# A pair's block sums of v, copied out of PSUM and spread over v's rows in the pair's first or second slot

## The chip, the cores and the metric

The kernel runs on one core of one Trainium2 chip. A time is the device time of one execution in microseconds (us), and the figure that counts is the median of several executions.

The engines are named as the profile names them: PE (TensorE, matrix multiplications; PEld is its loading of weights), DVE (VectorE), ACT (ScalarE), POOL (GpSimd) and SP (SyncE, which only issues DMA transfers here). Each takes its instructions in the order in which the program lists them. An instruction that needs another engine's result waits at the head of its queue, and all that stands behind it on that engine waits too.

## The reference

Attention comes first: each query sees a window of its neighbours and, beside them, one summary of each block of 32 keys. A block's value summary is the mean of its 32 rows of v. Two feed-forward stages follow.

```
k_sum = k.reshape(B, H, nb, block, D).max(axis=3)      # block = 32
v_sum = v.reshape(B, H, nb, block, D).mean(axis=3)
...
scores_all = np.concatenate([scores_l_m, scores_s], axis=-1)
...                                                     # softmax -> a
v_all = np.concatenate([v, v_sum], axis=2)
return np.matmul(a, v_all)                              # _attn_ref
...
h = x @ w_in                                            # _moe_ref, 512 -> 2048 -> 512
g = np.where(h > 0.0, h, np.exp(np.minimum(h, 0.0)) - 1.0)
x = g @ w_out
...                                                     # _moe2_ref: each token to one of 8 experts
```

The shapes are 2 batches, 8 heads, 768 tokens and 64 elements of a head; 1536 tokens of 512 elements go through the feed-forward stages.

## The kernel before

Attention is cut into **pairs** p of two heads and 384 tokens. There are 16 pairs, and each is worked in two **units** u of three query blocks of 64: units 2p and 2p+1. A **slot** `sl` of the main loop starts unit u = sl, so a pair has a first slot (even, `sl % GPP == 0`) and a second slot (odd). The order of instructions is the order in which the loop's body is written; no scheduler changes it.

The steps of a unit u are these. I write S3, T3 and so on for step and unit.

- S(u): `pe_s`, L280, PE: scores of 12 matmuls into PSUM; the keys `kw` and queries `qt` must be there.
- max(u): `dve_max`, L294, DVE: adds the mask and finds the row maxima, three instructions with a read of the result behind each.
- exp(u): `act_exp`, L301, ACT: three exponentials with their row sums.
- norm(u): L307 and L308 on DVE (the reciprocal of the row sums), then L309 on POOL, which multiplies.
- T(u): `pe_t`, L316, PE: three transposes of the result, one slot later.
- pT(u): `act_t`, L320, ACT: copies these out of PSUM, two slots after S(u).
- O(u): `pe_o`, L328, PE: probabilities times values, two slots after S(u). The values are the pair's tile `vw`: rows 0 to 95 are the windows of v, loaded by DMA (L187), and rows 96 to 119 are the block sums.
- copy of O(u): `act_o`, L339, ACT.

The block sums of a pair p come in four steps: `prep_va` (L222, DVE) sums blocks of v; V(p), `pe_va` (L230, PE), transposes the sums at the pair's first slot; `fin_va` (L236, ACT) copies them out of PSUM into `vs`, with the division by 32; `load_vs` (L242, POOL) spreads `vs` over the six windows of `vw`.

The first nine slots are the **prologue** (LAG = 9). In slots 0 to 7 the four pairs of the first 384 tokens are worked by attention alone, with some matmuls on the identity (`busy`, L884) between them. The last of these slots' work, O6 and O7, stands in slot 8, which already has the first matrix product of the feed-forward stage, `mm1(0, 0)` (L440), between S8 and O6. From slot 9 on each slot holds attention and feed-forward work.

In a prologue slot PE runs: S(u), V(p) if the slot is even, O(u-2), two `busy` matmuls, T(u-1). The lines that call the two steps in question, for pairs 1 to 3, are these; pair 0 has its own call in slot 1, and from pair 4 on `load_vs` is a DMA from a `vs` that is there already.

```
1200            if 0 < p < NPAIR and sl % GPP == 0:
1201                fin_va(p)                          # behind exp(u), ahead of the copy of O(u-2)
...
1245            if 0 < p < NPAIR and sl % GPP == 0:
1246                load_vs(p)                         # behind norm(u)
```

Of the kernel before, what the change touches and what calls it, by code (L numbers as in the profile page):

```python
# [22 lines left out]
NPAIR = NH // 2  # L23
# [26 lines left out]
def build(tc, cap, qT, kT, vT, vP, wi, wo, wg, wgT, wx, out):  # L50
# [6 lines left out]
    with ctx:  # L57
# [89 lines left out]
        GPP = QPT // GRP  # L147
# [84 lines left out]
        def fin_va(p):  # L232
            t, pr = divmod(p, NPAIR)
            if t % 2 == 0:
                VS[p] = apool.tile([P, P], F32, tag=f"vs{pr}", bufs=1, name=f"vs{p}")
                nc.scalar.mul(out=VS[p][WK:KEYS], in_=PS.pop(("v", p))[WK:KEYS], mul=1.0 / BLK)  # L236
            else:
                VS[p] = VS[p - NPAIR]

        def load_vs(p):  # L240
            if p < NPAIR:
                nc.gpsimd.tensor_copy(  # L242
                    out=VW[p][WK:KEYS], in_=VS[p][WK:KEYS].unsqueeze(1).to_broadcast([NSUM, QPT, P]))
                return
            nc.sync.dma_start(
                out=VW[p][WK:KEYS], in_=VS[p][WK:KEYS].unsqueeze(1).to_broadcast([NSUM, QPT, P]))
# [51 lines left out]
        def act_exp(u):  # L298
            sc, st = SC[u], ST[u]
            for gi in range(GRP):  # L300
                nc.scalar.activation(  # L301
                    out=sc[:, gi], in_=sc[:, gi], func=AF.Exp, bias=st[:, 0, gi : gi + 1],
                    scale=-1.0, accum_out=st[:, 1, gi : gi + 1])

        def norm(u):
            sc, st = SC[u], ST.pop(u)
            nc.vector.tensor_scalar(out=st[:, 2], in0=st[:, 1], scalar1=1e-9, scalar2=None, op0=ALU.add)  # L307
            nc.vector.reciprocal(out=st[:, 2], in_=st[:, 2])  # L308
            nc.gpsimd.tensor_tensor(  # L309
                sc, sc, st[:, 2].unsqueeze(2).to_broadcast([P, GRP, KEYS]), op=ALU.mult)  # L310
# [638 lines left out]
        for sl in range(total):  # L949
            n = sl - LAG  # L950
            u, p = sl, sl // GPP
# [245 lines left out]
            if u < NU:  # L1197
                dve_max(u)
                act_exp(u)
            if 0 < p < NPAIR and sl % GPP == 0:  # L1200
                fin_va(p)
            if sl == 0:
                prep_va(0)
# [38 lines left out]
                dve_o(u - 2)  # L1242
            if u < NU and not dense:
                norm(u)
            if 0 < p < NPAIR and sl % GPP == 0:
                load_vs(p)
            if sl in (LAG - 3, LAG - 2):
                w_conv([("i", sl - LAG + 3)], (2,))
# [291 lines left out]
```

## Time and profile before

| what | value |
|---|---|
| median of 3 runs | 494.66 us (494.08 to 495.25) |
| profiled execution, its own time | 495.4 us |
| its span, first to last instruction | 493.7 us |
| PE busy | 468.8 us (95%) |
| DVE busy | 333.7 us (68%) |
| ACT busy | 262.7 us (53%) |
| POOL busy | 189.5 us (38%) |
| mean granted clock of TensorE | 0.996 |

The profile is of one execution. The busy shares are averages over stages of different kinds, and the change touches only the first 30 us, so what matters is the timelines of that stretch, engine by engine: when each instruction starts, how long it runs, and in brackets how long its engine stood idle before it and what ended that.

### The profile page before, as it was taken

To read this page: it belongs to the slowest core of one execution; us is meant where nothing else is said; L and a number is where in the kernel's file an instruction comes from. 1 tells how busy PE (TensorE), PEld (TensorE's weight loads), DVE (VectorE), ACT (ScalarE), POOL (GpSimd) and SP (SyncE) were. 2 spreads that over 40 slices of the span, in tenths; PEclk is the share of its full clock that TensorE was granted. 3 is DMA by queue.
4 is the path that set the end of the run, shared out by engine and by line. 5 is a ranking of instruction groups with operands and counts; after the bars stand their busy time and mean duration, and the time that the engine had idled before them with its cause. 6 is when DMAs were issued, how large, how long until landed. Compare 5 with 4: busy or idle time off the path is not lost. (4 is left out here: it accounts for less than half of the span.)

```text
span 493.7 us, 9010 instructions
## 1 busy us (share of the span) xinstructions
PE 468.8 (95%) x2982; PEld 390.5 (79%) x2982; DVE 333.7 (68%) x889; ACT 262.7 (53%) x661; POOL 189.5 (38%) x197
## 2 busy tenths in 40 slices
PE   6999999999999999999999999999989999999983
PEld 5655555788888899998999899989768889798762
DVE  4869999666755477885279889756695846265550
ACT  4756446777665555564333333425734856376440
POOL 5632444555333358886233233123523040120430
PEclk9999999999999999999999999999999999999998
DMA  8996774433522433486010100106628875376570
GB/s 256 289 306 183 222 219 119 123 105 85 161 82 88 145 113 116 141 322 231 0 65 2 61 5 1 65 0 218 184 69 280 260 245 179 109 238 194 155 254 13
DMA packets 33729, 72.85 MB, mean 148 GB/s; under 512 B 4156, under 2 KB 9212, under 8 KB 33648
## 3 DMA queue, kind: packets, MB, share of 16 engines
q1 hardware_dynamic: 31888, 66.71, 42.7%
q0 software_dynamic: 1760, 5.19, 3.4%
q8 instruction: 34, 0.56, 0.5%
q14 instruction: 47, 0.39, 0.2%
HBM read 61.88 MB, written 9.70 MB: 145 GB/s over the span
## 5 line engine op out<-in xcount | busy, mean ns | idle before, releaser
L447 PE MATMUL h<-xT,Wi 128*128 128x384 f32 x672 | 130.3, 340 | 0.0
L492 PE MATMUL acc<-Wo,g 128*128 128x512 f32 x504 | 127.0, 396 | 0.2 <-POOL g L472 0.2
L447 PEld LDWEIGHTS h<-xT,Wi 128*128 128x128 f32 x672 | 118.0, 188 | 5.8 <-issue 1.9
L472 POOL TENSOR_TENSOR g<-e,g 128x384 fp32r<-128x384 f32 x55 | 65.0, 1182 | 127.9 <-ACT g L466 127.9
L492 PEld LDWEIGHTS acc<-Wo,g 128*128 128x128 f32 x504 | 92.9, 188 | 17.9 <-POOL g L472 0.7
L459 DVE SCALAR_TENSOR_TENSOR e<-e,h 128x384 f32<-128x384 f32 x64 | 35.3, 552 | 50.8 <-ACT e L455 47.4
L454 ACT ACTIVATE e<-h 128x384 f32<-128x384 f32 x64 | 31.5, 492 | 57.7 <-PE h L447 54.0
L466 ACT CAST g<-e 128x384 fp32r<-128x384 f32 x56 | 28.8, 514 | 45.8 <-DVE e L459 45.8
L684 DVE TENSOR_TENSOR E<-rawq,E 128x512 fp32r<-128x512 f32 x70 | 46.5, 706 | 8.5 <-ACT E L674 7.2
L816 PE MATMUL bh<-xbq,E 128*128 128x256 f32 (+1 forms) x288 | 43.5, 303 | 3.4 <-DVE tabs L1388 1.4
L674 ACT CAST E<-rawq 128x512 fp32r<-128x512 f32 x75 | 42.3, 617 | 6.5 <-DMA rawq<-wx 3.4
L816 PEld LDWEIGHTS bh<-xbq,E 128*128 128x128 f32 x288 | 41.2, 188 | 5.8 <-issue 1.7
L301 ACT ACTIVATE sc<-sc,st 128x120 f32<-128x120 f32 x96 | 36.7, 385 | 13.9 <-DVE st L294 13.8
L309 POOL TENSOR_TENSOR sc<-sc,st 128x360 f32<-128x360 f32 x32 | 27.9, 872 | 38.1 <-DVE st L308 26.0
L805 PE MATMUL y<-E,g 128*128 128x512 f32 x168 | 41.7, 393 | 0.0
L554 DVE CUSTOM_DVE_ANT_0 dot<-a,wgb 128x512 f32<-128x512 f32 x48 | 40.0, 887 | 0.0
L805 PEld LDWEIGHTS y<-E,g 128*128 128x128 f32 x168 | 30.6, 188 | 5.7
L455 ACT ACTIVATE e<-e 128x384 f32<-128x384 f32 x64 | 33.6, 525 | 2.0
L294 DVE CUSTOM_DVE_ANT_0 sc<-S,masks 128x120 f32<-128x120 f32 x96 | 21.5, 278 | 16.4 <-PE S L269 9.2
L320 ACT COPY pT<-T 120x384 f32<-120x384 f32 x32 | 15.3, 479 | 30.7 <-PE T L316 29.4
L824 DVE TENSOR_TENSOR g<-e,g 128x256 fp32r<-128x256 f32 (+1 forms) x24 | 11.3, 470 | 25.3 <-ACT g L823 21.0
L721 POOL DMA_INDIRECT out<-ys,sidx x6 | 6.3, 1052 | 48.2 <-ACT ys L720 46.7
(251 smaller groups left out, 694.4 us busy)
## 6 DMA issues: line engine op xcount, KB each, us to landing
rawq<-wx SPq DMA_DIRECT2D x88, 256.0 KB, 3.9
rawi<-wi SPq DMA_DIRECT2D x16, 512.0 KB, 3.7
rawo<-wo SPq DMA_DIRECT2D x16, 512.0 KB, 6.2
vw<-vP SPq DMA_DIRECT2D x16, 288.0 KB, 3.0
qt<-qT SPq DMA_DIRECT2D x16, 192.0 KB, 3.7
vt<-vT SPq DMA_DIRECT2D x8, 384.0 KB, 3.1
out<-xg SPq DMA_DIRECT2D x12, 256.0 KB, 4.8
x2d<-a SPq DMA_DIRECT2D x12, 256.0 KB, 4.2
```

The source lines that it names most:

```text
L301: nc.scalar.activation(out=sc[:, gi], in_=sc[:, gi], func=AF.Exp, bias=st[:, 0, gi : gi + 1], scale=-1.0, accum_out=st[:, 1, gi : gi + 1])
L447: nc.tensor.matmul(HP[t, f][:, 0:TT], lhsT=w[:, s, c * P : (c + 1) * P], rhs=xT[t][:, xs, c, :], start=c == 0 and n == 0, stop=c == NCC - ...
L454: nc.scalar.activation(out=e, in_=HP[t, f][:, 0:TT], func=AF.Exp)
L455: nc.scalar.activation(out=e, in_=e, func=AF.Relu, bias=1.0, scale=-1.0)
L459: nc.vector.scalar_tensor_tensor(out=e, in0=e, scalar=-1.0, in1=h[:, 0:TT], op0=ALU.mult, op1=ALU.max)
L472: eng.tensor_tensor(g[:, 1], EP.pop((t, f)), g[:, 0].bitcast(F32), op=ALU.subtract)
L492: nc.tensor.matmul(accp[tb], lhsT=g[:, s, tb * P : (tb + 1) * P], rhs=w[:, ws], start=f % FPG == 0 and n == 0, stop=f % FPG == FPG - 1 and ...
L554: nc.vector.tensor_tensor_reduce(out=junk, in0=x2[t * BPT + tb], in1=WGB[e // 2][:, e % 2], scale=1.0, scalar=0.0, op0=ALU.mult, op1=ALU.a ...
L674: (nc.vector.tensor_copy if m in vec else nc.scalar.copy)(EW[k][m][:, 0], raw_of(k, m))
L684: (nc.gpsimd if m in pool else nc.vector).tensor_tensor(w[:, 1], raw, w[:, 0].bitcast(F32), op=ALU.subtract)
L805: nc.tensor.matmul(ys[b], lhsT=g[:, s, b * P : (b + 1) * P], rhs=w[:, ws], start=f == 0 and n == 0, stop=f == 7 and n == 2)
L816: nc.tensor.matmul(h[:, 0:nt], lhsT=EW[k][half * NCC + c][:, ws, fc * P : (fc + 1) * P], rhs=xb[:, s, c, 0:nt], start=n == 0, stop=n == 3 ...
```

## The change

For pairs 1, 2 and 3 both calls get the condition `sl % GPP == 1` in place of `sl % GPP == 0`. The pair's first slot keeps V(p).

```diff
-            if 0 < p < NPAIR and sl % GPP == 0:
+            if 0 < p < NPAIR and sl % GPP == 1:
                 fin_va(p)
...
-            if 0 < p < NPAIR and sl % GPP == 0:
+            if 0 < p < NPAIR and sl % GPP == 1:
                 load_vs(p)
```

No instruction is added or removed, and no DMA is moved: for these pairs `fin_va` is one instruction on ACT and `load_vs` one on POOL. Three of each move.

On POOL, around the first slot of pair 1 (`sc` is a unit's probabilities, `kw` the keys of the pair after, `vw` the pair's values), the order before is:

```order
L309 TENSOR_TENSOR sc_272<-sc_272,st_273 128x360
L242 COPY vw_198<-vs_280 24x768
L309 TENSOR_TENSOR sc_328<-sc_328,st_329 128x360
L197 COPY kw_377<-kt_238 128x6x64
L199 COPY kw_377<-kt_238 128x6x32
L216 COPY kw_377<-ks_380 128x6x24
L309 TENSOR_TENSOR sc_366<-sc_366,st_367 128x360
```

The three products on L309 are norm 2, norm 3 and norm 4. At the same place on POOL, the changed kernel has:

```order
L309 TENSOR_TENSOR sc_272<-sc_272,st_273 128x360
L309 TENSOR_TENSOR sc_325<-sc_325,st_326 128x360
L242 COPY vw_198<-vs_333 24x768
L197 COPY kw_375<-kt_238 128x6x64
L199 COPY kw_375<-kt_238 128x6x32
L216 COPY kw_375<-ks_378 128x6x24
L309 TENSOR_TENSOR sc_366<-sc_366,st_367 128x360
```

The spread over `vw` has gone behind norm 3, the product of the pair's second unit; the copies of keys now follow it.

PE's order is the same in both kernels. In the changed one, around the start of slot 4 (V(2), then O2, which reads the `vw` above, then T3 and S5), with the engines that each waits for:

```order
L230 MATMUL V_355<-ident,va_126 120x128 [waits DVE_49]
L328 MATMUL O_359<-pT_357,vw_198 64x64 [waits DMAHW2_49,Activation_49,Pool_49]
L328 MATMUL O_359<-pT_357,vw_198 64x64 x5
L884 MATMUL warm<-ident 128x128 x2
L316 MATMUL T_389<-ident,sc_325 120x128 [waits PE_49]
L316 MATMUL T_389<-ident,sc_325 120x128 x2
L280 MATMUL S_393<-kw_282,qt_225 64x120 [waits DVE_49,PE_49]
```

What moved is what O2's wait for POOL stands for: the spread is POOL's instruction ahead of norm 3 before, and the one behind it now. T3, which waits for norm 3, stands behind O2 in both and no longer has a wait of its own for POOL.

On ACT the copy `vs` (L236) leaves its place between exp 2 and the copy of O0 and stands between exp 3 and the copy of O1; likewise for pairs 2 and 3.

## Rows read from the trace of the kernel before

**Rows 1.** Page, part 1: busy time and share of the span by engine.
```profile
PE 468.8 (95%) x2982; PEld 390.5 (79%) x2982; DVE 333.7 (68%) x889; ACT 262.7 (53%) x661; POOL 189.5 (38%) x197
```

**Rows 2.** Busy us of PE, PEld, DVE, ACT, POOL by stretch; PE's clock, DMA share, GB/s.
```profile
10.00:20.00 10.00, 8.70 (x109) 6.23 (x108) 7.93 (x33) 7.25 (x32) 6.99 (x13) 1.00 1.04 323
...
40.00:50.00 10.00, 10.00 (x65) 5.63 (x62) 9.95 (x29) 6.82 (x24) 3.14 (x4) 1.00 0.66 202
```

**Rows 3.** Timeline of PE: start us, us, instruction, [idle before it, releaser].
```profile
14.35 0.83 PE L280 MATMUL S<-kw,qt 64*64 64x120 f32 x12
...
17.44 0.33 PE L230 MATMUL V<-ident,va 128*120 128x128 f32 x1
17.69 0.57 PE L328 MATMUL O<-pT,vw 120*64 120x64 f32 x12
...
18.47 0.49 PE L316 MATMUL T<-ident,sc 128*120 128x128 f32 x3
18.89 0.83 PE L280 MATMUL S<-kw,qt 64*64 64x120 f32 x12
...
22.84 0.57 PE L328 MATMUL O<-pT,vw 120*64 120x64 f32 x12
...
24.04 0.83 PE L280 MATMUL S<-kw,qt 64*64 64x120 f32 x12
...
25.45 0.57 PE L328 MATMUL O<-pT,vw 120*64 120x64 f32 x12 [0.21 <-ACT pT L320]
...
26.42 0.55 PE L316 MATMUL T<-ident,sc 128*120 128x128 f32 x3
26.90 0.83 PE L280 MATMUL S<-kw,qt 64*64 64x120 f32 x12
27.66 2.20 PE L440 MATMUL h<-x,T 128*128 128x384 f32 x6
29.80 0.57 PE L328 MATMUL O<-pT,vw 120*64 120x64 f32 x12
```

**Rows 4.** Timeline of POOL, slots 2 to 7.
```profile
15.82 0.82 POOL L242 COPY vw<-vs 24x768 f32<-24x768 f32 x1
17.49 0.79 POOL L309 TENSOR_TENSOR sc<-sc,st 128x360 f32<-128x360 f32 x1 [0.85 <-ACT pT L320]
...
25.32 1.05 POOL L309 TENSOR_TENSOR sc<-sc,st 128x360 f32<-128x360 f32 x1 [1.61 <-DVE st L308]
26.43 0.92 POOL L242 COPY vw<-vs 24x768 f32<-24x768 f32 x1
28.36 1.05 POOL L309 TENSOR_TENSOR sc<-sc,st 128x360 f32<-128x360 f32 x1 [1.00 <-DVE st L308]
```

**Rows 5.** Timeline of DVE: unit 3, and a conversion of weights in slot 7.
```profile
15.34 0.28 DVE L294 CUSTOM_DVE_ANT_0 sc<-S,masks 128x120 f32<-128x120 f32 x1 [0.55 <-PE S L280]
...
17.14 0.18 DVE L308 RECIPROCAL st<-st 128x3 f32<-128x3 f32 x1
...
28.10 0.66 DVE L423 SCALAR_TENSOR_TENSOR T<-rawi,T 128x512 uint32<-128x512 uint32 x1
```

**Rows 6.** Timeline of ACT: the copy `vs` and pT of slots 2 and 5, unit 3's exponentials.
```profile
14.39 0.27 ACT L236 ACTIVATE vs<-V 24x128 f32<-24x128 f32 x1
...
15.66 0.40 ACT L301 ACTIVATE sc<-sc,st 128x120 f32<-128x120 f32 x1 [0.28 <-DVE st L294]
...
16.72 0.18 ACT L301 ACTIVATION_READ_ACCUMULATOR sc<-sc,st 128x1 f32 x1
...
19.77 0.48 ACT L320 COPY pT<-T 120x384 f32<-120x384 f32 x1
```

**Rows 7.** Timeline of PE: O3 (slot 5) and the start of slot 9.
```profile
20.31 0.57 PE L328 MATMUL O<-pT,vw 120*64 120x64 f32 x12 [0.22 <-ACT pT L320]
...
36.33 2.85 PE L440 MATMUL h<-x,T 128*128 128x384 f32 x8 [0.31 <-DVE e L459]
```

**Rows 8.** Waits of PE from 46 us to the end, longest first: us, times, longest.
```profile
PE ht_0z L750 <- ACT hs_0z L745: 2.3, 1, 2.3
```

**Rows 9.** As rows 2: two stretches of the prologue, two of the end.
```profile
10.00:12.00 2.00, 1.30 (x16) 0.91 (x15) 1.31 (x3) 1.26 (x6) 1.58 (x2) 1.00 1.03 395
12.00:14.00 2.00, 1.39 (x18) 0.89 (x17) 1.97 (x10) 0.87 (x5) 0.97 (x2) 1.00 1.06 252
...
488.00:490.00 2.00, 0.00 (x0) 0.00 (x0) 0.00 (x0) 0.00 (x0) 0.00 (x0) 0.87 0.04 5
490.00:494.00 4.00, 0.00 (x0) 0.00 (x0) 0.00 (x0) 0.00 (x0) 0.00 (x0) 0.50 0.04 10
```

## The prediction

> **What bounds the kernel now.** I read the busy shares first: PE is busy for 468.8 of 493.7 us [rows 1], so the kernel as a whole waits for PE. But the change touches only slots 2 to 7, about 11 to 27 us, and there the busy table by stretch says something else. Between 10 and 20 us no engine is full: PE 8.70, DVE 7.93, ACT 7.25, POOL 6.99 of 10 us [rows 2]. A stretch like that is bound by a chain that passes from engine to engine, and it must be read instruction by instruction. From slot 9 on PE has no gap (10.00 of 10 us from 40 to 50 us [rows 2]), so a delay that reaches PE there should run through to the end.
>
> So I follow unit 3, the second unit of pair 1, through the timelines. S3 starts on PE at 14.35 [rows 3], its maximum on DVE at 15.34, the exponentials on ACT at 15.66, the last sum is read at 16.72 + 0.18 = 16.90 [rows 6], the reciprocal starts at 17.14 [rows 5], and norm 3 starts on POOL at 17.49 and ends at 18.28 [rows 4]. The row of norm 3 names ACT's pT as what ended its wait; the reciprocal ended at 17.32, 0.17 us ahead of it, and is what it really waits for. **From the start of S3 to the end of norm 3 it is 3.93 us.** Nothing in this chain waited for the spread of `vs` over `vw`: that ran from 15.82 to 16.64 on POOL and left a gap of 0.85 us [rows 4]. The reader is to see two things. The spread was done 1.05 us before O2 began at 17.69, and O2 followed V(2) back to back (0.25 us from start to start) [rows 3]: before, the spread was on no critical path.
>
> **The change, part by part.** *What it takes away.* On ACT, 0.27 us of `vs` leaves the place ahead of the copy of O and of pT in each first slot of a pair [rows 6]. That can help PE where it waited for pT: O3 waited 0.22 us and O5 0.21 us for it [rows 3, 7]. If that were all, the gain would be at most 3 x 0.27, and by the two waits some 0.4 us. On POOL, the even unit's product stays where it was and the odd unit's product loses a predecessor it did not wait for: nothing.
>
> *What it adds.* The copy `vs` goes behind exp of the odd unit on ACT, which delays that slot's copy of O and pT by 0.27 us; O of the even unit, which reads that pT, now waits longer for something else, so I cost this at nothing. The spread goes behind norm of the odd unit on POOL, and O of the even unit, one slot later, reads `vw`. So O2 waits for norm 3. Behind O2 in PE's queue stand T3 and S5, and S5 is the head of the next pair's chain. A loop is closed that was open before: S3, max, exp, norm 3, spread, O2, T3, S5.
>
> *The length of the loop.* From S3 to the end of norm 3 it is 3.93 us. The spread starts 0.07 us behind a product on POOL (an estimate from norm 6, which ends at 25.32 + 1.05 = 26.37, and the spread behind it at 26.43 [rows 4]) and takes 0.82 [rows 4]; PE starts some 0.07 us after what it waits for (O3 at 20.31, its pT done at 19.77 + 0.48 = 20.25 [rows 6, 7]). That makes 4.89 us from S3 to O2. From O2 to S5 it is 18.89 - 17.69 = 1.20 us [rows 3]. **One turn is 6.09 us**, where before S3 to S5 took 4.54 and S5 to S7 5.15 [rows 3].
>
> *The sum.* S3 itself keeps its time: nothing ahead of it changes but the 0.27 us on ACT.
> - Pair 1: O2 starts at 14.35 + 4.89 = 19.24 instead of 17.69, 1.55 us late. S5 starts at 20.44.
> - Pair 2: O4 starts at 20.44 + 4.89 = 25.33 instead of 22.84, 2.49 us late. S7 starts at 26.53 instead of 24.04.
> - Pair 3 ends in slot 8, where the first feed-forward product fills PE between S8 and O6. Before, S7 to O6 took 29.80 - 24.04 = 5.76 us [rows 3]. Of this 0.21 us at O5 was a wait; T6 began 0.97 us behind O5 and S8 0.48 us behind T6, where T3 began 0.78 us behind O2 and S5 0.42 us behind T3, so 0.25 us more were waits for the first half of the pair [rows 3]. After the change that work has long been done, and 5.3 us remain, which puts PE at O6 at 31.83. The spread of pair 3 ends at 26.53 + 3.93 + 0.07 + 0.82 = 31.35, and with the longer product and spread seen in slots 6 and 7 (1.05 and 0.92 instead of 0.79 and 0.82 [rows 4]) at 31.71. POOL and PE arrive there together; with the conversions that DVE has in front of that unit's reciprocal I add 0.1 us. **O6 starts at about 31.9 instead of 29.80: 2.1 us late.**
>
> From O6 on all of slot 8 hangs on PE, and slot 9 begins with a wait for DVE of 0.31 us [rows 7] whose own input comes from PE, so it moves along. After that I find no slack that could take the 2.1 us back: the longest wait of PE behind 46 us, 2.3 us, is for ACT in the last expert [rows 8], and that too is fed by work that starts later.
>
> Against the profiled execution this is 495.4 + 2.1 = 497.5 us (span 493.7 + 2.1 = 495.8, and the same 1.7 us around it). That execution lies 0.74 us above the median of 494.66, so against the median I forecast **496.8 us**, 0.42% slower.
>
> *Bounds.* The low end is what pair 1 alone gives, 1.5 us, if the two later pairs get back 0.6 us through earlier copies on ACT. The high end takes 1.05 and 0.92 for every product and spread, which adds 0.36 us to each of two turns: 2.8 us.
>
> *A rule weighed against a row.* POOL's products are not all alike: 0.79 us at 17.49, but 1.05 us at 28.36, where DVE ran a conversion of 0.66 us from 28.10 [rows 4, 5]. So a neighbour on DVE costs POOL 0.1 to 0.26 us here. The Trainium skill, "SBUF — State Buffer", section "Who interferes with whom", states that a DVE instruction with two SBUF inputs and a GpSimd instruction that reads SBUF exclude each other, and that the later one is blocked for the whole instruction. By that rule a spread of pair 3 that begins just behind a conversion would stand for up to 0.66 us, and the sum would be 2.8; by the rows it is 2.1 to 2.4.
>
> **The rivals.**
> *A, the spread is in time after all and ACT's earlier pT shows (not slower).* Its place is O2: the spread would have to end by 17.6. The mechanism is the freed ACT: pT of unit 1 comes 0.27 us earlier. It decides only if norm 3 ended before 16.7, and that would need 1.6 us less in a chain that ends at 18.28 [rows 4]. The price is a gain of about 0.4 us: 494.2 us, no change to measure. Only a misreading of the order would bring it about. 4%.
> *B, the delay is given back later (not slower to measure).* Two microseconds are lost at slot 8, but the transfers of the prologue, which keep the DMA engines full (share 1.04 [rows 2]), get ahead, and a later wait that depends on them shrinks. For it speaks that the last long wait of PE is 2.3 us [rows 8]. Against it: no wait of PE from 46 us on names a DMA as its releaser, and PE is full from 40 us. If half comes back it is 495.7, if nearly all 494.9 us. 10%.
> *C, PE's clock falls.* O2 and O4 make PE idle for about 1.5 us each. The granted clock is 1.00, the level of 2.4 GHz, in all stretches of the prologue, also between 10 and 14 us where PE was busy for 1.30 and 1.39 of 2 us; only at the end, after PE had stopped for good, it falls to 0.87 and then to 0.50, which is 1.2 GHz [rows 9]. At 0.50 PE's share of a turn, 1.20 us behind O and 0.99 from S to DVE, would double: 2.2 us for each of two turns, 4.4 us, hence 501.2 us. 6%. The Trainium skill, "TensorE: Matmul & The Clock Gate", section "A second HAM failure mode: psum-queue depth-cycling", tells of a kernel whose clock swung because PE idled briefly and often between groups of matmuls. By that rule rival C is what happens here; the rows between 10 and 14 us do not bear it out.
>
> **How the numbers follow.** The forecast itself, 1.5 to 2.8 us later, has 80%: 496.2 to 497.5. The 0.2% that a measurement of this kernel can tell from no change are 1.0 us, so all of it is slower. A (4%) is no change, B (10%) mostly no change, C (6%) slower. Slower is then 80 + 6 = 86%, of which I move 4 to "no change", since the three runs before spread over 1.2 us. Faster, by an unseen gain over 1 us, keeps 3%: slower 0.82, same 0.15, faster 0.03. The range goes from half given back, 495.5, to the high bound with some scatter of the median, 497.9.
>
> **What would show it.** In the timeline of PE after the change, O2 must start near 19.2, O4 near 25.3 and O6 near 31.9, the first two with a wait of about 1.5 us put down to POOL's spread, and with V(2) and V(3) back to back behind S4 and S6. POOL must show norm 3 and the spread back to back, norm 3 still at 17.49. S5 and S7 should start 1.55 and 2.49 us later. From slot 9 on all instructions should start some 2.1 us later, and the clock should stay at 1.00. I am wrong if O2 starts before 18 us, if slot 9 starts within 1 us of its old time, or if the shift is there at 40 us and gone at the end.

## The result and the profile after

The changed kernel takes 499.52 us (median of 8, 496.49 to 504.17) against 494.88 us (median of 8): a ratio of 1.0083, 95% interval 1.0056 to 1.011. Beside the second set of experiments it was run again and gave 499.47 against 495.82 us, a ratio of 1.0091 (1.0056 to 1.0126). So it is slower, as forecast, but not by 2.1 us: by the medians it is 4.6 and 3.7 us, by the ratios 4.1 and 4.5 us, and both intervals begin at 2.8 us. The range ended at 497.9.

The first profile fell on the slowest of its executions (504.17 us), which the ratio leaves out, so the rows below are from the second comparison's profile (499.28 us, span 497.5), which I call the changed kernel's. In it the program starts slot 3 later than the profile of before did, S3 at 15.41 instead of 14.35. S0 and S1, which stand ahead of all that moved, ran at half speed here (1.47 and 1.42 us instead of 0.83); in a second profile of before S0 took 1.46 us as well. I therefore measure all places from S3, and take the start of slot 9's first product (the row of 36.33 in [rows 7]) as the end of the stretch: 21.98 us after S3 before, and 22.12 in that second profile.

PE's timeline of the changed kernel, to be read against [rows 3]:

```profile
15.41 0.83 PE L280 MATMUL S<-kw,qt 64*64 64x120 f32 x12
...
18.50 0.33 PE L230 MATMUL V<-ident,va 128*120 128x128 f32 x1
20.28 0.57 PE L328 MATMUL O<-pT,vw 120*64 120x64 f32 x12 [1.46 <-POOL vw L242]
20.78 0.57 PE L884 MATMUL warm<-ident 128*128 128x128 f32 x2
21.14 0.85 PE L316 MATMUL T<-ident,sc 128*120 128x128 f32 x3
21.92 1.47 PE L280 MATMUL S<-kw,qt 64*64 64x120 f32 x12
...
27.57 0.57 PE L328 MATMUL O<-pT,vw 120*64 120x64 f32 x12 [1.17 <-POOL vw L242]
...
28.76 0.83 PE L280 MATMUL S<-kw,qt 64*64 64x120 f32 x12
...
34.08 0.57 PE L328 MATMUL O<-pT,vw 120*64 120x64 f32 x12
...
40.61 2.85 PE L440 MATMUL h<-x,T 128*128 128x384 f32 x8 [0.31 <-DVE e L459]
```

Two things are to be seen. O2 now waits 1.46 us for the spread and starts 20.28 - 15.41 = 4.87 us after S3; the sum said 4.89. And behind that wait PE's instructions take longer for the same work: T3 0.85 us instead of 0.49, S5 1.47 us instead of 0.83. POOL's timeline, against [rows 4], shows norm 3 and the spread back to back:

```profile
18.55 0.79 POOL L309 TENSOR_TENSOR sc<-sc,st 128x360 f32<-128x360 f32 x1 [1.74 <-DVE st L308]
19.41 0.82 POOL L242 COPY vw<-vs 24x768 f32<-24x768 f32 x1
```

The table by stretch says why PE is slow (columns as in [rows 2]; the number ahead of the last two is PE's granted clock):

```profile
18.00:20.00 2.00, 0.82 (x13) 0.47 (x9) 1.62 (x9) 1.91 (x8) 1.38 (x2) 1.00 0.99 250
20.00:22.00 2.00, 1.72 (x19) 1.32 (x21) 0.95 (x3) 0.62 (x3) 1.94 (x5) 0.74 1.01 268
22.00:24.00 2.00, 2.00 (x16) 1.37 (x18) 0.46 (x3) 0.61 (x2) 0.08 (x1) 0.50 0.46 173
24.00:26.00 2.00, 2.00 (x30) 1.67 (x29) 1.51 (x7) 1.95 (x9) 0.16 (x1) 0.91 0.19 30
26.00:28.00 2.00, 0.83 (x17) 0.56 (x13) 1.67 (x8) 1.40 (x7) 1.88 (x3) 1.00 0.93 283
```

From 18 to 20 us PE was busy for 0.82 of 2 us; then the clock fell to 0.50, the level of 1.2 GHz, until about 24 us. Slot 9 begins 40.61 - 15.41 = 25.20 us after S3, 3.22 us later than before (21.98). In the first profile of the same kernel the fall came behind the second wait, from 26 to 30 us, and the stretch took 25.61 us, 3.63 more.

### The profile page after: what moved, and what is told of

The parts are those of the page before. It is cut to its first block, busy times and chain, and to the rows that moved or that the text cites. A ratio compares the mean times of both kernels' runs of the same rounds, so it can differ in the third digit from the quotient of the medians.

```text
span 502.4 us, 9005 instructions
## 1 busy us (share of the span) xinstructions
PE 475.0 (95%) x2982; PEld 395.5 (79%) x2982; DVE 335.9 (67%) x889; ACT 263.2 (52%) x661; POOL 190.0 (38%) x197
## 5 line engine op out<-in xcount | busy, mean ns | idle before, releaser
L684 DVE TENSOR_TENSOR E<-rawq,E 128x512 fp32r<-128x512 f32 x70 | 48.1, 728 | 9.0 <-ACT E L674 7.8
L816 PE MATMUL bh<-xbq,E 128*128 128x256 f32 (+1 forms) x288 | 45.1, 310 | 3.5 <-DVE tabs L1388 1.4
L816 PEld LDWEIGHTS bh<-xbq,E 128*128 128x128 f32 x288 | 42.8, 196 | 5.8 <-issue 1.7
L309 POOL TENSOR_TENSOR sc<-sc,st 128x360 f32<-128x360 f32 x32 | 27.9, 872 | 42.1 <-DVE st L308 27.2
L320 ACT COPY pT<-T 120x384 f32<-120x384 f32 x32 | 15.3, 479 | 31.9 <-PE T L316 30.6
```

What stands on the lines that cost most here:

```text
L684: (nc.gpsimd if m in pool else nc.vector).tensor_tensor(w[:, 1], raw, w[:, 0].bitcast(F32), op=ALU.subtract)
L816: nc.tensor.matmul(h[:, 0:nt], lhsT=EW[k][half * NCC + c][:, ws, fc * P : (fc + 1) * P], rhs=xb[:, s, c, 0:nt], start=n == 0, stop=n == 3 ...
```

## The experiments

Two theories could explain the miss. The first: the loop through O costs its 2.1 us, and the rest is TensorE's clock, which falls behind the idle stretches that the loop opens. The rival: the chain is longer than costed, or the change costs something else.

**Fill the idle stretches.**

```diff
             if sl < LAG - 1 and sl % GPP == 0 and p:
                 pe_va(p)
+                if sl in (4, 6):
+                    busy(10)
```

> The changed kernel with ten more matmuls on the identity on PE between V(p) and O of the even unit, in slots 4 and 6, where PE otherwise idles for 1.5 us. They cost some 0.134 us each (8 took 1.07 us in the prologue of before), so they end before the spread does and lengthen nothing. Theory (the loop through O costs 2.1 us, the rest of the 4.6 us is TensorE's clock falling behind these idle stretches): the granted clock stays at 1.00 from 18 to 32 us, O2 and O4 still wait for the spread, and the time is 496.5 to 497.5. Rival (the clock falls elsewhere or for another reason; the chain itself is longer than costed): the time stays near 499.5.

Measured: 496.96 against 495.98 us, ratio 1.002 (1.0002 to 1.0039). PE's timeline:

```profile
14.66 0.83 PE L280 MATMUL S<-kw,qt 64*64 64x120 f32 x12
...
17.91 1.26 PE L884 MATMUL warm<-ident 128*128 128x128 f32 x10
19.54 0.57 PE L328 MATMUL O<-pT,vw 120*64 120x64 f32 x12 [0.37 <-POOL vw L242]
...
32.33 0.57 PE L328 MATMUL O<-pT,vw 120*64 120x64 f32 x12
...
38.86 2.85 PE L440 MATMUL h<-x,T 128*128 128x384 f32 x8 [0.32 <-DVE e L459]
```

The stretches of the two waits, columns as above:

```profile
18.00:20.00 2.00, 1.63 (x23) 1.36 (x21) 1.96 (x8) 1.49 (x7) 1.88 (x4) 1.00 0.98 260
...
24.00:26.00 2.00, 1.41 (x15) 1.17 (x16) 1.92 (x8) 1.58 (x7) 1.85 (x3) 1.00 0.83 259
```

The granted clock is 1.00 in every stretch from 4 to 40 us, O2 still waits for the spread, and slot 9 begins 24.20 us after S3: 2.22 us more than before. Work that computes nothing and shortens no chain gives back 1.0 us of the 3.22, or 1.4 of the 3.63 of the first profile, within the prologue. The theory holds for the profile, and the time is in the expected range. But by the interval it is 0.1 to 1.9 us above before, less than the loop's 2.2. Before's executions beside it had the lower mean clock (0.9928 against 0.9939), which may be part of that; it is not shown.

**Only the spread moves**, the copy out of PSUM stays in the first slot.

```diff
-            if 0 < p < NPAIR and sl % GPP == 1:
+            if 0 < p < NPAIR and sl % GPP == 0:
                 fin_va(p)
```

> Only the spread over vw (POOL) moves to the pair's second slot; the copy out of PSUM (ACT) stays in the first. Theory (the spread behind the odd unit's norm is what closes the loop, ACT's place is worth nothing): as the changed kernel, 498 to 501, O2 with the same wait of about 1.5 us for the spread. Rival (ACT's copy behind the odd unit's exponentials matters as well): clearly less than the changed kernel, 495 to 497.

Measured: 499.17 us, ratio 1.0062 (1.0037 to 1.0088). O2 waits 1.46 us for the spread, O4 1.69 us, the clock is at 0.50 from 26 to 28 us, and slot 9 begins 25.66 us after S3. That is the first profile of the changed kernel again (25.61 us): ACT's copy has no part in it. Against the fill, on the same chip and in the same comparison, it is 2.2 us slower by the medians.

```profile
26.00:28.00 2.00, 2.00 (x19) 1.54 (x17) 1.56 (x5) 0.50 (x2) 1.59 (x3) 0.50 0.97 333
```

**O one slot later**, so that it no longer stands ahead of the next pair's scores.

```diff
+            if sl in (5, 7):
+                pe_o(u - 3)
+                act_o(u - 3)
             if u - 2 in late:
                 act_t(u - 2)
-                if u != NU:
+                if u != NU and sl not in (4, 6):
                     pe_o(u - 2)
...
-            if u - 2 in late and u != NU:
+            if u - 2 in late and u != NU and sl not in (4, 6):
                 act_o(u - 2)
```

> The changed kernel with O2 and O4 (and the copies of them) one slot later, behind S5 and S7 on PE, so that what waits for the spread no longer stands ahead of the next pair's scores. Theory (a closed loop S, max, exp, norm, spread, O, T, S): the loop is open again, S5 and S7 start within 0.4 us of their places in the kernel before, O6 waits for the last spread until about 30.5 instead of 29.8, the clock stays at 1.00, and the time is 495.2 to 496.2. Rival (it is the spread's place on POOL or the wait itself that costs, wherever O stands): near 499.5.

Measured: 497.15 us, ratio 1.0034 (1.001 to 1.0057). S5 starts 4.47 us after S3 (4.54 before) and S7 9.99 us (9.69 before): the loop is open, as expected. The clock held. But O6 is 1.42 us late relative to S3, twice what I had expected: O3 and O5 each wait 0.80 us for pT, since the copy of O2 or O4, which is late, now stands ahead of pT on ACT. Part of the wait was moved, not removed: slot 9 begins 23.41 us after S3, 1.43 us late, and the time is 1.7 us above before by the ratio, more than I had expected (495.2 to 496.2).

**The kernel before without its fill in slots 2 to 7.**

```diff
-            elif sl < LAG - 1:
-                busy(2 if p else 4)
+            elif sl < 2:
+                busy(4)
...
-            if sl < LAG - 1:
-                busy(2 if p else 4)
+            if sl < 2:
+                busy(4)
```

> The kernel before, without the matmuls on the identity in slots 2 to 7 (those ahead of and in slots 0 and 1 stay), so that PE idles in the prologue while the order of all else, the spread too, is that of before. Theory (TensorE's clock falls when PE idles in this stretch, and that costs some 2 to 4 us): granted clock below 0.9 in some stretch from 14 to 32 us in most executions, time 496 to 499. Rival (the clock holds, the idle does no harm): 494 to 495.

Measured: 497.49 us, ratio 1.004 (1.0011 to 1.007). The time fits the theory, the profile doesn't: slot 9 begins 21.64 us after S3, even 0.34 us earlier than before, and the clock is 1.00 up to 400 us, also from 24 to 26 us, where PE was busy for only 0.79 of 2 us. A second profile was taken to see where this kernel loses:

> The kernel before without the matmuls on the identity in slots 2 to 7, one more profile of it. Theory (its loss of some 2 us is the clock falling in the prologue of some executions): a granted clock below 0.9 in a stretch from 14 to 32 us, if this execution's mean clock is at 0.992 or lower. Rival (its clock falls late, in the experts): 1.00 up to 40 us.

That execution took 499.54 us, and the rival held: the clock was 1.00 up to 400 us and fell in the experts.

```profile
400.00:440.00 40.00, 37.69 (x200) 34.43 (x200) 19.82 (x34) 22.60 (x45) 7.29 (x7) 0.96 0.53 168
440.00:470.00 30.00, 26.81 (x149) 22.45 (x148) 18.18 (x30) 17.25 (x36) 5.14 (x5) 0.99 0.58 184
470.00:480.00 10.00, 10.00 (x43) 8.17 (x42) 6.46 (x11) 5.24 (x10) 4.43 (x4) 0.86 0.67 201
```

So PE's many short idle times in this prologue, each under 0.9 us, did not bring the clock down in two profiles, and my theory was wrong on this kernel. The rival was wrong as well in holding that the idle does no harm: the kernel is slower, and why its clock falls late is open.

**The kernel before with more fill early**, and **the changed kernel with both fills**.

```diff
-        busy(16)
+        busy(20)
...
+            if sl == 2:
+                busy(4)
             if sl < LAG - 1 and sl % GPP == 0 and p:
                 pe_va(p)
...
-                busy(2 if p else 4)
+                busy(2 if p else 9 if sl else 4)
```

> The kernel before with more matmuls on the identity where PE idles early: four more ahead of slot 0, five more at the end of slot 1, four ahead of V(1) in slot 2. The order of all else is that of before. Single executions of the kernel before differ by up to 6 us and their mean granted clock between 0.988 and 0.996. Theory (the clock of the prologue falls in some executions of the kernel before too, behind these early gaps): the mean granted clock rises and the median is 0.5 to 1.5 us lower than that of before. Rival (the spread of before comes from later stages alone): within 0.3 us of before.

> The changed kernel with both fills, the early ones and the ten matmuls ahead of O in slots 4 and 6, so that PE has no idle stretch over 0.8 us in the prologue. Theory (what is left is the loop through O alone): 2.0 to 2.4 us above the kernel before with the early fill, granted clock 1.00 in the whole prologue. Rival (part of the chain's 2.1 us is taken back later): 1.0 to 1.4 us above it.

Measured: the first 494.68 us against 495.82, but the ratio is 0.9996 (0.9963 to 1.003), so it can't be told from before, and the mean granted clock of its executions did not rise (0.9935 against 0.9936): that theory is not borne out. The second took 497.93 us, ratio 1.0045 (1.0017 to 1.0072), and slot 9 begins 24.20 us after S3, as in the fill alone: 2.22 us more than before, clock 1.00. Above the kernel with the early fill it is 3.25 us by the medians and 2.4 by the ratios; I had expected 2.0 to 2.4. In the same comparison, the changed kernel itself:

> The changed kernel itself once more, beside the kernels above on one chip. Theory (2.1 us from the loop, 1.4 us from the clock between O4 and S8): 3 to 4.5 us above before; its profile shows a granted clock of 0.5 somewhere between 24 and 31 us and slot 9 begins 3.3 to 3.8 us later than before relative to S3. Rival (the fall of the clock in the first profile was that execution's own): clock 1.00 from 14 to 32 us.

Measured as told above: 499.47 us, the clock at 0.50, slot 9 3.22 us late. The fall came earlier than I had expected, behind O2 and not between 24 and 31 us, and slot 9 was just short of the 3.3 to 3.8. The two fills are worth 1.5 us by the medians and 2.3 us by the ratios, whose intervals overlap.

**One pair alone.**

```diff
-            if 0 < p < NPAIR and sl % GPP == 0:
+            if 0 < p < NPAIR and sl % GPP == (p == 3):
```

(at both calls; the other kernel has `p == 1`)

> Only pair 3's copy and spread move to its second slot. Theory: no next pair hangs on it, so only O6 waits for the spread behind norm 7, until about 30.5 instead of 29.8 on the clock of the profile of before (or 0.5 to 1.0 us later relative to S7); PE idles there for under 1 us and the clock holds; the time is 0.4 to 1.2 us above before. Rival (each moved pair costs a third of the whole): 1.2 to 1.6 us above before.

> Only pair 1's copy and spread move to its second slot. Theory (one turn of the loop, then the old order, in which O4 waits for nothing new): O2 waits some 1.5 us and S5 is 1.55 us late relative to S3, but S7 only 0.9 us, since O3, T4 and S6 had waits that this hides; slot 9 begins 0.5 to 0.9 us later relative to S3 than before if the clock holds, and 1.0 to 1.5 us more if it falls. Rival (each delay of PE adds in full): 1.5 us.

Measured for pair 3: 496.32 us, ratio 1.0011 (0.9984 to 1.0039), no difference that can be told, and slot 9 at 21.86 us after S3, 0.12 us earlier than before. S7 to O6 took 5.96 instead of 5.76 us, so O6 does wait for the spread, but for less than the 0.5 to 1.0 us expected: where the spread used to stand, DVE gained. In the kernel before, DVE's conversion of slot 7 ran beside it:

```profile
26.70 1.20 DVE L420 SCALAR_TENSOR_TENSOR T<-rawi,T 128x512 uint32<-128x512 uint32 x1
```

and with pair 3's spread moved away the same conversion is done sooner, and with it norm 7:

```profile
26.27 0.69 DVE L420 SCALAR_TENSOR_TENSOR T<-rawi,T 128x512 uint32<-128x512 uint32 x1
...
28.81 1.19 DVE L420 SCALAR_TENSOR_TENSOR T<-rawi,T 128x512 uint32<-128x512 uint32 x1
```

The 0.5 us has gone to the next conversion, in slot 8, beside which the spread now runs. The Trainium skill, "SBUF — State Buffer", section "Who interferes with whom", says that a DVE instruction with two SBUF inputs contends with a GpSimd instruction that reads SBUF, and that the order of issue decides which of the two blocks. The trace agrees with the order: the spread starts first, at 26.43, and takes 0.92 instead of 0.82 us; DVE starts at 26.70 and takes 1.20 instead of 0.69.

Measured for pair 1: 496.46 us, ratio 1.002 (1.0003 to 1.0037). O2 waits 1.46 us, S5 starts 6.07 us after S3, S7 10.68 us (9.69 before), slot 9 23.11 us: 1.13 us late. That lies between the 0.5 to 0.9 I expected and the rival's 1.5. The clock held in this profile, though PE was busy for only 0.55 of 2 us from 18 to 20 us:

```profile
18.00:20.00 2.00, 0.55 (x13) 0.48 (x13) 1.95 (x8) 1.68 (x8) 1.88 (x4) 1.00 1.07 272
```

**The spread in two halves**, the even unit's windows first.

```diff
-                nc.gpsimd.tensor_copy(
-                    out=VW[p][WK:KEYS], in_=VS[p][WK:KEYS].unsqueeze(1).to_broadcast([NSUM, QPT, P]))
+                for g in range(GPP):
+                    nc.gpsimd.tensor_copy(
+                        out=VW[p][WK:KEYS, g * GRP : (g + 1) * GRP],
+                        in_=VS[p][WK:KEYS].unsqueeze(1).to_broadcast([NSUM, GRP, P]))
```

> The changed kernel with the spread in two instructions of three windows each, the even unit's windows first, so that O of the even unit waits for the first half alone. Theory (the spread is one term of the loop): each turn is shorter by a half spread, 0.41 us less a start of some 0.07, so the wait ahead of O2 is 1.1 instead of 1.46 us, and slot 9 begins 1.4 to 1.6 us later relative to S3 than before, not 2.2, where the clock holds. Rival (O waits for the whole tile): 2.2 us or more.

Measured: 498.79 us (4 runs), ratio 1.0066 (1.0042 to 1.009).

```profile
14.17 0.83 PE L282 MATMUL S<-kw,qt 64*64 64x120 f32 x12
...
18.73 0.57 PE L330 MATMUL O<-pT,vw 120*64 120x64 f32 x12 [1.14 <-POOL vw L243]
...
19.92 0.83 PE L282 MATMUL S<-kw,qt 64*64 64x120 f32 x12
...
25.08 0.57 PE L330 MATMUL O<-pT,vw 120*64 120x64 f32 x12 [1.75 <-POOL vw L243]
...
26.80 1.47 PE L282 MATMUL S<-kw,qt 64*64 64x120 f32 x12
```

O2 waits 1.14 us instead of 1.46, and the first turn takes 5.75 us instead of 6.07: the spread is a term of the loop, and O waits for its half alone. The rest can't be compared (slot 9 begins 25.37 us after S3), since the second pair of halves took 1.50 us instead of 0.95 and the clock fell behind O4.

**The kernel before, once more.**

> The kernel before, one more profile of it. Theory (in its own order the clock holds from slot 2 on): granted clock 1.00 from 14 to 40 us, slot 9 begins 21.6 to 22.2 us after S3; S0 may run at 1.2 GHz, as in two profiles of the changed order. Rival (the clock falls in the prologue of before as often): below 0.9 somewhere from 14 to 32 us.

Measured: 494.75 us; S0 took 1.46 us, the clock was 1.00 from 10 to 470 us, slot 9 began 22.12 us after S3. The theory holds.

## Why the prediction was wrong

*What bounds the prologue* was read rightly. The chain from S3 over norm 3 to the spread is what the trace after shows, and it is the spread's place behind norm 3 that closes the loop (only the spread moved: the same loss; O out of the way: S5 and S7 back at their places).

*The loop's sum* was right to 0.2 us in each part. Where the clock held (both fills), S3 to S5 took 6.07 us (forecast 6.09), S5 to S7 6.30 (6.09), S7 to O6 5.30 (5.3), and O6 came 17.67 us after S3 (31.9 - 14.35 = 17.55). Slot 9 was 2.22 us late; the forecast was 2.1. Halving the spread shortened the first turn by 0.32 us.

*The gain on ACT* was costed at nothing in the sum, rightly: with ACT's copy in its old place the stretch is the same to 0.1 us (25.66 against 25.61 us, both with the clock's fall behind O4).

*The step that failed is rival C, the clock.* The sum put it at nothing, and I gave it 6%, on the ground that PE had been busy for only 1.30 and 1.39 of 2 us in two stretches of before with the clock at 1.00 [rows 9]. The loop makes PE busy for 0.65 to 0.83 of 2 us in the stretches of its waits, and no row of the prologue of before shows so little behind the start. I took the nearest row as if it covered the case. What the runs showed: in all four profiles of kernels in which the waits ahead of both O2 and O4 stand unfilled (the change twice, the spread alone, the halved spread) the clock fell to 0.50 behind one of the two waits, and not behind the other. In both profiles of before, in the filled kernels, with O one slot later, with one pair moved alone and in the kernel without fill it held up to 40 us.

A row of the late stages would not have settled it either. There the trace of before has a wait of PE that is longer than any ahead of O2 or O4 in these runs, the 2.3 us of [rows 8], and the clock read 1.00 around it (the row of PE, then the table by stretch):

```profile
477.05 0.66 PE L750 MATMUL ht_0z<-ident,hs_0z 128*128 128x128 f32 x4 [2.29 <-ACT hs_0z L745]
```

```profile
460.00:480.00 20.00, 17.57 (x84) 13.78 (x83) 13.63 (x21) 10.53 (x20) 9.27 (x7) 1.00 0.73 233
```

So one execution in which the clock holds behind a wait does not show that it will hold in the next. The Trainium skill, "TensorE: Matmul & The Clock Gate", section "A second HAM failure mode: psum-queue depth-cycling", tells of a kernel whose clock swung because PE idled briefly and often between groups of matmuls. The trace agrees in part: the clock fell to 0.50 from 22 to 24 us, but once and behind one long wait, while the kernel without fill, with many short idle times, held 1.00 there.

*Its price* was wrong too. I had 4.4 us on top of 2.1, from two whole turns at half speed. The clock falls once in the prologue and for between 3 and 4 us, and that costs 1.0 (25.20 against 24.20 us) to 1.4 us (25.61) within the prologue; with the spread alone it is 1.5 (25.66). So 2.2 + 1.0 to 1.4 = 3.2 to 3.6 us are shown in the timelines of the changed kernel, of 4.1 to 4.5 measured by the ratios.

*What stays open.* The 0.5 to 1.3 us between the two are not located, and they may be nothing, since both intervals reach down to 2.8 us. From slot 9 to the end of the span, profiles in which the clock held there took 455.8 to 457.4 us, and five in which it fell somewhere between 360 and 480 us took 458.3 to 462.0 us; kernels whose prologue kept its clock are among these five (pair 3 alone, and the one without fill, twice). The first profile of the changed kernel is one, the second is not. Of all executions the mean granted clock is on record. It is 0.9906 over the ten of the changed kernel in the second comparison, against 0.9936 for before and 0.9929 with both fills, and 0.9939 with the fill alone, against 0.9928 for before beside it. A fall to 0.50 for 3 to 4 us takes 0.003 to 0.004 off the mean of a span of 497.5 us (an estimate from the table by stretch), so the gap is of the size of the one fall in the prologue, and the fill closes it. But the mean does not say where the clock fell: the kernel without fill has 0.9907, with no fall in the prologue of its two profiles. Whether the changed kernel has late falls more often than before is therefore not shown. Nor did I settle why one idle stretch of 1.46 us brought the clock down in one execution of the changed kernel and not in the other, nor in that of pair 1 alone.

*Rivals A and B* did not come about: O2 did not start in time, and nothing of the shift was taken back that the rows show: from slot 9 to the end of the span the changed kernel's second profile took 456.9 us, the two of before 457.4 and 456.4.

## What to carry to other kernels

Before a step is moved to a later slot, look for who reads its result and what stands behind that reader on its own engine: a copy that waited for nothing can close a loop when it goes behind the last step of the stage that feeds it. Then ask what the reader's engine does while it waits; if that is TensorE, price the clock's fall as a likely case, not as a remote one, even where the one trace at hand shows as long a wait at full clock. Filler matmuls in that wait gave the clock's part back here, and only that.

## What the runs showed of the hardware that I had not expected

Waits of PE for the spread, 1.1 to 1.8 us long, were followed by a fall of the granted clock to 0.50 for between 3 and 4 us in four of eight cases, and the ninth, in the kernel with pair 1 alone, was not. PE was busy again when the clock fell: in the changed kernel O2 ran at its usual 0.57 us at 20.28, and only T3 behind it took 0.85.

The clock column is not complete at the start of a program: in the second profile of before S0 took 1.46 us instead of 0.83, while the table gave 1.00 for that stretch. In the changed kernel S5 took 1.47 us at 0.50.

```profile
5.90 1.46 PE L280 MATMUL S<-kw,qt 64*64 64x120 f32 x12 [0.47 <-DMA qt<-qT]
```

Executions of one and the same kernel on one core differ by some 6 us (493.74 to 499.74 for before in one comparison). Where two profiles of one kernel lie apart, most of it is behind slot 9, where the clock fell somewhere between 360 and 480 us: 3.6 of 3.8 us without fill, 4.7 of 4.9 us in the changed kernel.
